# Linear attention into a Swish feed-forward block: one output tile moved ahead of a batch's key-value products, one weight load and one minimum cut in two

## The chip, the cores and the metric

The kernel runs on one NeuronCore of a Trainium2 chip. The metric is the device time of one launch in microseconds (us). A core has five engines that run their own instruction streams and meet only at semaphores: TensorE (PE; its weight loads are shown apart as PEld), VectorE (DVE), ScalarE (ACT), GpSimd (POOL) and SyncE (SP). Transfers are issued by SP, ACT and POOL. TensorE writes into PSUM, which here is cut into banks of 128 x 512 float32; the other engines copy from there to SBUF.

## The reference

```python
def _attn_ref(q, k, v):                      # 8 batches, 8 heads, 576 rows, 64 columns
    def phi(x):
        return np.where(x > 0, x, np.exp(x) - 1.0) + 1.0
    q_p, k_p = (phi(q), phi(k))
    kv = np.einsum('bhsd,bhse->bhde', k_p, v)
    z = np.sum(k_p, axis=2)
    num = np.einsum('bhsd,bhde->bhse', q_p, kv)
    den = np.einsum('bhsd,bhd->bhs', q_p, z)[..., None] + 1e-06
    return (num / den).astype(np.float32)

def _moe_ref(x, w_in, w_out, beta):          # x: 4608 x 512, d_ff = 2048
    h = x @ w_in
    g = h * (1.0 / (1.0 + np.exp(-beta * h)))
    return (g @ w_out).astype(np.float32)
```

The attention's output, its heads side by side, is the x of the second function. Each batch gives 576 rows: 512 of them make four tiles of 128, and the 64 that are left over (the "odd" rows) of all eight batches are gathered in a ninth block.

## The kernel before

**Stages.** For each of nine blocks of 512 rows the kernel runs an h phase (16 products of 128 columns of w_in with xT, the transposed x of the block, each into its own PSUM bank, each followed by Silu on ACT into g) and a y phase (four output tiles, t = 0 to 3; each sums 16 matmuls of g with w_out in one bank). Beside the phases of block b the attention of a later batch is computed. From batch 2 on this is hung between the matmuls by the tables `sh` and `sy`; batches 0 and 1 are written out by hand, and the change lies there. `tc.manual_schedule()` is set: every engine executes its instructions in the order of the program's text.

**phi.** phi(x) = min(exp(x), max(x, 0) + 1). `phi_part` takes exp on ACT (`e`, four buffers), `phi_relu` the other side on DVE (`r`), `phi_min` the minimum on DVE. `phi_step` calls these for batch 0, with an optional range j0:j1 of the nine row groups.

**Batch 0, up to about 20 us.** q and k are loaded, phi is taken, q is transposed on PE (`q_trans`, copied out by `q_copy`). `z_products` sums phi(k), `kv_direct` makes k^T v, `kv_evac` and `diagonal` copy it out on DVE and ACT, `z_evac` copies z. `numer_mm` makes the numerators in tiles of the pool `num0ps` (two buffers, which z uses first), `x_part` transposes x, and `h0_part` is the h phase's first quarter in pieces; it needs the first quarter of w_in.

**Loads.** POOL issues the loads that change the type from float32 to bfloat16: k and v of batch 0 in halves, w_in in four quarters (L119, L120), then w_out in four quarters, q, k, v of batch 1, and q (`xq`), k (`xk`) and v of batch 2. All of them are in POOL's one queue in this order.

**Batch 1, about 30 to 49 us.** Block 0's y phase holds all four banks of the pool `mmps` as `yps[0]` to `yps[3]`. Its matmuls come in quarters i = 0 to 3 of d_ff (`y_mm(0, t, i, ...)`), with batch 1's attention between: `z_products`, `z_evac`, `kv_direct`, `kv_evac`, `dens`, `numer0` and `x_trans1`. The last quarter, i = 3, is what lies between the pieces of attention (L769 to L781):

```python
    y_mm(0, 0, 3, yps[0])
    for t in range(4):
        numer0(1, t, num0_tile() if t < 2 else miscps.tile([P, 512], F32, tag="misc", name="nps1"))
    ...
    for t in (1, 2):
        for i in range(2):
            y_mm(0, t, 3, yps[t], 256 * i, 256 * (i + 1))
            x = 2 * (t - 1) + i
            x_trans1(x, nc.scalar if x < 3 else nc.vector)
    y_mm(0, 3, 3, yps[3])
```

On ACT the order there is: `phi_part(2, "q", 0)` (exp of the first half of batch 2's q, L768), the copies of x_trans1(0) to (2), exp of both halves of batch 2's k, exp of the second half of q, the table load for Silu, and the Silus of block 1. On DVE: the four scalings of `numer0`, the copy of x_trans1(3), then `y_out` of tiles 0 to 2, `phi_relu` of k, `y_out` of tile 3, and the minima. `y_out` copies a bank to one of three buffers `y_sb` and issues two output transfers of 128 KB on SP.

**Block 1's h phase.** Products 0, 1, 2 and 6 go into the banks of `mmps` that `yps` gave back, 5 into that of product 0, 3 and 4 into the pool `numps` (two buffers, `h_ps2`). Product 6 is followed by `q_odd_trans(1, num_tile("qop"))` (L847): two transposes of batch 1's odd rows into the `numps` buffer of product 3, so that PE must wait for the Silu of product 3.

Of the kernel before, what the change touches and what calls it, by code (L numbers as in the profile page):

```python
# [16 lines left out]
def kernel(  # L17
# [10 lines left out]
    nc = tc.nc  # L28
# [8 lines left out]
    J = S // G  # L37
# [18 lines left out]
    w_in_sb = [consts.tile([P, KC, 512], BF16, name=f"w_in{i}") for i in range(4)]  # L56
# [59 lines left out]

    w_in_v = moe_w_in.rearrange("(c p) f -> p c f", p=P)
    w_out_v = moe_w_out.rearrange("(c p) m -> p c m", p=P)
    for i in range(4):  # L119
        nc.gpsimd.dma_start(out=w_in_sb[i], in_=w_in_v[:, :, i * 512 : (i + 1) * 512])  # L120

    def load_w_out(i):
# [17 lines left out]
    def phi_part(b, a, pr, x, j0=0, j1=J):  # L140

        if j0 == 0:
            st[b, a, pr, "e"] = work.tile([P, 2, J, D], BF16, tag="e", name="e", bufs=4)
        nc.scalar.activation(st[b, a, pr, "e"][:, :, j0:j1], x[:, :, j0:j1], ACTF.Exp)  # L144

    def phi_relu(b, a, pr, x):
        r = work.tile([P, 2, J, D], BF16, tag="r", name="r", bufs=2)
        nc.vector.tensor_scalar(r, x, 0.0, 1.0, ALU.max, ALU.add)  # L148
        st[b, a, pr, "r"] = r
# [16 lines left out]
    def xin(b, a, pr):  # L166
        if b == 0 and a == "q":
            return q0f[:, places(b, pr)]
        return (xk if a == "k" else xq)[b % NX][:, places(b, pr)]
# [7 lines left out]
    def k_quads(b, pr, dst, mov):  # L177

        for j in range(J):
            for h in range(2):  # L180
                for hh in range(2):
                    r = slice(hh * G, (hh + 1) * G)
                    c = slice(h * D, (h + 1) * D)
                    nc.tensor.matmul(  # L184
                        dst[hh][c], st[b, "k"][r, pr, j, c], mov(r, j, h),
                        start=(j == 0), stop=(j == J - 1), skip_group_check=True,
                    )

    def z_products(b, pr, ps):

        for j in range(J):
            for hh in range(2):
                r = slice(hh * G, (hh + 1) * G)
                nc.tensor.matmul(
                    ps[hh][:, 256 + pr : 257 + pr], st[b, "k"][r, pr, j, :], ones[r, 0:1],
                    start=(j == 0), stop=(j == J - 1), skip_group_check=True,
                )

    def z_evac(b, ps):
        for hh in range(2):  # L200
            nc.vector.tensor_mul(
                z0[:, hh], ps[hh][:, 256:258, None].to_broadcast([P, 2, 2]),
                kvmask[:, :, :, 0],
            )

        nc.gpsimd.tensor_copy(
            st[b, "kv"].rearrange("p x a (h e) -> p (x a h) e", h=2)[:, :, D],
            z0.rearrange("p x a h -> p (x a h)"),
        )

    def kv_direct(b, pr, ps):
        k_quads(
            b, pr, [a[:, pr * D : (pr + 1) * D] for a in ps],
            lambda r, j, h: vb[b][r, 2 * pr + h, j, :],
        )

    def kv_evac(b, hh, prs, ps):
        p0, p1 = prs[0], prs[-1] + 1
        nc.vector.tensor_mul(
            st[b, "kv"][:, hh, p0:p1].rearrange("p a (h e) -> p a h e", h=2)[:, :, :, 0:D],  # L220
            ps[hh][:, p0 * D : p1 * D].rearrange("p (a d) -> p a d", a=p1 - p0)[
                :, :, None, :
            ].to_broadcast([P, p1 - p0, 2, D]),
            kvmask[:, p0:p1, :, 0:D],
        )
# [15 lines left out]
    def copy(eng, dst, src):  # L241
        if eng is nc.scalar:
            nc.scalar.copy(dst, src)
        else:
            eng.tensor_copy(dst, src)  # L245

    def q_copy(b, k, t, tp, eng):
        slots = 1 if t == NT - 1 else 2
        tp = tp.rearrange("p (t a h i g) -> p t a h i g", a=2, h=2, i=slots, g=G)
        copy(  # L250
            eng,
            st[b, "qT"][:, t, :, :, 0 : slots * G].rearrange("p a h n -> p (a h) n"),
            tp[:, k].rearrange("p a h i g -> p (a h) (i g)"),
        )
# [170 lines left out]
    def x_trans(b, t, eng, tp):  # L425
        n = P if t < NT - 1 else G
        xv = st[b, "xs", t].rearrange("p i a d -> p (i a d)")
        tp = tp[:, 0 : KC * P].rearrange("p (c t) -> p c t", c=KC)
        for p in range(KC):
            nc.tensor.matmul(  # L430
                tp[:, p, :n], xv[:n, p * P : (p + 1) * P], identity[:n, :n],
                is_transpose=True, start=True, stop=True, skip_group_check=True,
            )
        if eng is nc.scalar:
            nc.scalar.copy(x_dst(b, t), tp[:, :, :n])  # L435
        else:
            eng.tensor_copy(x_dst(b, t), tp[:, :, :n])
# [28 lines left out]
    def mm_tile(name):  # L466
        return mmps.tile([P, 512], F32, tag="mm", name=name)

    def y_mm(b, t, i, yp, c0=0, c1=512):
        for c in range(4):  # L470
            ff = 4 * i + c
            nc.tensor.matmul(  # L472
                yp[:, c0:c1],
                g_sb[b % 2][:, ff, t * P : (t + 1) * P],
                w_out_sb[i][:, c, c0:c1],
                start=(ff == 0), stop=(ff == FC - 1), skip_group_check=True,
            )

    def rows(b, j):
        return out[b * S : (b + 1) * S, :].rearrange("(g j) m -> j g m", j=J)[j]  # L480

    def y_out(b, t, yp, c0=0, c1=512, queues=(nc.sync, nc.sync), copier=nc.vector):
        y_sb = work.tile([P, DM], F32, tag="y_sb", name="y_sb", bufs=3)
        copy(copier, y_sb[:, c0:c1], yp[:, c0:c1])
        for i in range(2):
            dst = rows(b, 2 * t + i) if b < B else rows(2 * t + i, J - 1)
            queues[i].dma_start(out=dst[:, c0:c1], in_=y_sb[i * G : (i + 1) * G, c0:c1])
# [48 lines left out]
    def misc_bf():  # L536
        return miscps.tile([P, 1024], BF16, tag="misc", name="tp")
# [18 lines left out]
    def num0_tile():  # L556
        return num0ps.tile([P, 512], F32, tag="num0", name="nps0")
# [15 lines left out]
    def phi_step(a, pr, f, *r):  # L573
        f(0, a, pr, *((xin(0, a, pr),) if f is not phi_min else ()), *r)
# [18 lines left out]
    phi_step("q", 1, phi_min, 0, 4)  # L593
    phi_step("q", 1, phi_min, 4, J)
    phi_step("k", 0, phi_part)
    phi_step("k", 1, phi_part)
    tps = [misc_bf() for _ in range(2)]
    for i in range(2):
        q_trans(0, (2 * i, 2 * i + 1), tps[i], ())
# [1 line left out]
    q_copy(0, 0, 0, tps[0], nc.vector)  # L601
    phi_step("k", 0, phi_min)
    phi_step("k", 1, phi_relu)
    q_copy(0, 1, 1, tps[0], nc.vector)
    phi_step("k", 1, phi_min)
    for t in (2, 3):
        q_copy(0, t - 2, t, tps[1], nc.scalar)
    nc.scalar.activation(tiny[:, 1:2], warm[:, 0:1], ACTF.Silu)
# [72 lines left out]
    def diagonal(b, hh, p0, ps):  # L681

        for h in range(2):
            r = slice(h * D, (h + 1) * D)
            nc.scalar.copy(
                st[b, "kv"][r, hh, p0:2, h * EA : h * EA + D],
                ps[hh][r, p0 * D : 2 * D].rearrange("p (a d) -> p a d", d=D),
            )
# [52 lines left out]
    yps = [mm_tile("y_ps") for _ in range(4)]  # L741
# [14 lines left out]
    for pr in range(2):  # L756
        z_products(1, pr, zt1)
    z_evac(1, zt1)
    for pr in range(2):
        kv_direct(1, pr, kv1)  # L760
    kv_evac(1, 0, (0, 1), kv1)
    diagonal(1, 1, 0, kv1)
    dps1 = miscps.tile([P, 512], F32, tag="misc", name="dps1")
# [2 lines left out]
    phi_tile(2, "q")  # L766
    phi_tile(2, "k")
    phi_part(2, "q", 0, xin(2, "q", 0))  # L768
    y_mm(0, 0, 3, yps[0])  # L769
    for t in range(4):  # L770
        numer0(1, t, num0_tile() if t < 2 else miscps.tile([P, 512], F32, tag="misc", name="nps1"))

    def x_trans1(t, eng=nc.scalar):
        x_trans(1, t, eng, num0_tile().bitcast(BF16) if t < 2 else misc_bf())

    for t in (1, 2):
        for i in range(2):
            y_mm(0, t, 3, yps[t], 256 * i, 256 * (i + 1))
            x = 2 * (t - 1) + i
            x_trans1(x, nc.scalar if x < 3 else nc.vector)  # L780
    y_mm(0, 3, 3, yps[3])  # L781
    for pr in range(2):
        phi_part(2, "k", pr, xin(2, "k", pr))
    phi_part(2, "q", 1, xin(2, "q", 1))
    for t in range(3):
        y_out(0, t, yps[t])
    for pr in range(2):
        phi_relu(2, "k", pr, xin(2, "k", pr))
    y_out(0, 3, yps[3])
    for pr in range(2):  # L790
        phi_min(2, "k", pr)
    for pr in range(2):
# [110 lines left out]
```

## Time and profile before

| what | before |
|---|---|
| median of 13 runs | 285.74 us (285.27 to 287.99) |
| the profiled execution's own time | 285.39 us |
| its span in the profile | 283.6 us |
| PE busy, matmuls / weight loads | 274.9 us (97%) / 139.2 us (49%) |
| DVE / ACT / POOL busy | 106.4 (38%) / 160.6 (57%) / 36.8 us (13%) |
| granted TensorE clock, mean | 0.999 |
| DMA | 41.03 MB, mean 145 GB/s |

The span is what the profile shows of the execution; 1.8 us of the profiled execution's own time lie around it. Shares of busy time are means over stages with different limits. In the profile's lines a time is in us from the start of the span, "L472" is a line of the kernel, "y_ps<-w_out,g" says what is written from what, and "<-" in brackets names what ended an engine's idle time.

### The profile page before, as it was taken

What the parts mean: (1) busy time and instruction counts of PE and PEld (TensorE: products, weight loads), DVE (VectorE), ACT (ScalarE), POOL (GpSimd) and SP (SyncE); (2) the same over time, 40 slices, a digit from 0 to 9 for tenths busy, and PEclk for the clock granted to TensorE, in tenths of its full rate; (3) what the DMA queues carried; (4) which work ended last, traced back from release to release, by engine and by line L of the source; (5) the groups of instructions that cost most, each with busy time, mean ns of one, the idle gap of its engine ahead of it and who ended that gap; (6) DMA issues with size and microseconds to landing.
All of it is one profiled execution on the core that took longest, in us unless ns stands there. A gap on an engine that the chain in (4) does not pass through costs nothing.

```text
span 283.6 us, 5976 instructions
## 1 busy us (share of the span) xinstructions
PE 274.9 (97%) x2477; PEld 139.2 (49%) x2508; DVE 106.4 (38%) x260; ACT 160.6 (57%) x219; POOL 36.8 (13%) x51
## 2 busy tenths in 40 slices
PE   7899999999999999999999999999999999999994
PEld 2574457444854544454445444544444444444443
DVE  5842677806832474056404740371034100110012
ACT  5778586974786744893388528831750185028500
POOL 8722100314013002300040003000000000000000
PEclk9999999999999999999999999999999999999999
DMA  7999999669999938953998379166303510230033
GB/s 219 204 210 390 249 266 191 154 183 238 198 141 288 145 82 200 273 100 83 147 278 144 67 166 285 34 81 160 76 3 83 121 30 0 63 79 8 0 74 75
DMA packets 51723, 41.03 MB, mean 145 GB/s; under 512 B 31584, under 2 KB 43120, under 8 KB 51696
## 3 DMA queue, kind: packets, MB, share of 16 engines
q1 hardware_dynamic: 38800, 23.61, 36.1%
q0 software_dynamic: 12736, 16.91, 30.6%
q8 instruction: 19, 0.31, 0.5%
q10 hardware_dynamic: 160, 0.13, 0.2%
q14 instruction: 8, 0.07, 0.1%
HBM read 36.71 MB, written 9.44 MB: 163 GB/s over the span
## 4 chain that ended last, share of the span: by engine, by line
PE 81%; DMA 13%; POOL 2%; ACT 1%; issue 1%; DVE 0%; POOLq 0%; ACTq 0%
PE y_ps L472 39%; PE h_ps L454 39%; DMA xq<-in_q_dram 8%; DMA w_in<-in_moe_w_in_dram 5%; PE nps L184 1%; PE nps L309 1%; POOL w_in L120 1%; ACT e L144 1%; ACT xT L435 1%; POOL vf L83 1%; PE kvp L184 0%; PE nps_m L309 0%; POOL xk L83 0%; DVE y_sb L245 0%; POOL identity masks.py:199 0%
## 5 line engine op out<-in xcount | busy, mean ns | idle before, releaser
L462 ACT ACTIVATE g<-h_ps,beta_c 128x512 bf16<-128x512 f32 x144 | 97.8, 689 | 86.9 <-PE h_ps L454 86.4
L472 PE MATMUL y_ps<-w_out,g 128*128 128x512 bf16 (+3 forms) x615 | 125.9, 360 | 1.0 <-issue 0.2
L454 PE MATMUL h_ps<-xT,w_in 128*128 128x512 bf16 x487 | 108.5, 379 | 0.8 <-ACT e L144 0.3
L472 PEld LDWEIGHTS <-g 128*128 128x128 bf16 x632 | 60.7, 98 | 61.1
L454 PEld LDWEIGHTS <-w_in 128*128 128x128 bf16 x560 | 54.5, 98 | 65.5 <-DVE y_sb L245 0.7
L245 DVE COPY y_sb<-y_ps 128x512 f32<-128x512 f32 (+2 forms) x37 | 24.7, 672 | 81.2 <-PE y_ps L472 77.1
L392 DVE TENSOR_SCALAR den<-nps 128x12 f32<-128x12 f32 x12 | 2.0, 164 | 63.0 <-PE nps L309 63.0
L144 ACT ACTIVATE e<-xk 128x1152 bf16<-128x1152 bf16 x16 | 17.8, 1153 | 3.1 <-DVE phi_k L155 1.7
L83 POOL DMA_DIRECT2D xq<-in_q_dram x7 | 5.2, 747 | 89.1 <-DVE phi_k L155 41.8
L144 ACT ACTIVATE e<-xq 128x1152 bf16<-128x1152 bf16 x14 | 15.6, 1155 | 1.4 <-DMA xq<-in_q_dram 1.4
L454 PE MATMUL h_ps<-xT_tail,w_in 128*128 128x512 bf16 x62 | 13.9, 379 | 0.1
L173 POOL CAST vaug<-vf 128x1152 bf16<-128x1152 f32 x10 | 11.2, 1151 | 18.4 <-DMA vf<-in_v_dram 14.6
L155 DVE TENSOR_TENSOR phi_q<-e,r 128x1152 bf16<-128x1152 bf16 (+2 forms) x17 | 11.7, 716 | 2.7 <-ACT e L144 2.4
L383 DVE TENSOR_TENSOR xs<-nps,rden 128x512 bf16<-128x512 f32 (+1 forms) x24 | 12.2, 552 | 0.4
L144 ACT ACT_TABLE_LOAD x6 | 7.7, 1283 | 7.9 <-DMA xq<-in_q_dram 7.8
L155 DVE TENSOR_TENSOR phi_k<-e,r 128x1152 bf16<-128x1152 bf16 x16 | 11.7, 764 | 0.2
L133 PE MATMUL warm_ps<-xT 128*128 128x512 bf16 x20 | 7.5, 534 | 1.8 <-DVE xT L96 1.5
L462 ACT ACT_TABLE_LOAD x6 | 7.7, 1283 | 0.1
L83 POOL DMA_DIRECT2D xk<-in_k_dram x9 | 6.8, 758 | 4.6 <-DMA g<-in_moe_w_out_dram 2.0
L730 DVE TENSOR_SCALAR w_out<-g,rbeta 128x512 bf16<-128x512 f32 x8 | 3.8, 536 | 8.7 <-DMA g<-in_moe_w_out_dram 8.7
L184 PEld LDWEIGHTS <-phi_k 64*64 64x64 bf16 x576 | 5.6, 106 | 2.8 <-issue 2.1
L148 DVE TENSOR_SCALAR r<-xk 128x1152 bf16<-128x1152 bf16 x16 | 6.7, 453 | 0.0
(98 smaller groups left out, 118.1 us busy)
## 6 DMA issues: line engine op xcount, KB each, us to landing
out_dram<-y_sb SPq DMA_DIRECT2D x70, 128.0 KB, 2.4
vf<-in_v_dram SPq DMA_DIRECT2D x5, 1152.0 KB, 6.7
xq<-in_q_dram POOLq DMA_DIRECT2D x7, 576.0 KB, 10.1
xk<-in_k_dram POOLq DMA_DIRECT2D x7, 576.0 KB, 12.2
w_in<-in_moe_w_in_dram POOLq DMA_DIRECT2D x4, 512.0 KB, 12.8
g<-in_moe_w_out_dram POOLq DMA_DIRECT2D x2, 1024.0 KB, 17.8
stage<-in_moe_w_out_dram POOLq DMA_DIRECT2D x2, 1024.0 KB, 20.7
stage<-in_q_dram SPq DMA_DIRECT2D x2, 576.0 KB, 4.0
```

What stands on the lines that cost most here:

```text
L83: return eng.dma_start(out=dst[:, h0 : h0 + n].rearrange("p h j d -> p h (j d)"), in_=rows.rearrange("(i p) e -> p i e", p=P)[:, h0 : h0 + n],
L133: nc.tensor.matmul(warm_ps[:, 0:cols], warm[:, 0:P], warm[:, 0:cols], start=True, stop=True)
L144: nc.scalar.activation(st[b, a, pr, "e"][:, :, j0:j1], x[:, :, j0:j1], ACTF.Exp)
L148: nc.vector.tensor_scalar(r, x, 0.0, 1.0, ALU.max, ALU.add)
L155: nc.vector.tensor_tensor(st[b, a][:, pr, j0:j1].rearrange("p j (h d) -> p j h d", h=2), st[b, a, pr, "e"][:, :, j0:j1].rearrange("p h j d ...
L173: eng.tensor_copy(vaug[b % 2][:, pr, :, :, 0:D], src[:, places(b, pr)].rearrange("p h j d -> p j h d"))
L184: nc.tensor.matmul(dst[hh][c], st[b, "k"][r, pr, j, c], mov(r, j, h), start=(j == 0), stop=(j == J - 1), skip_group_check=True,)
L245: eng.tensor_copy(dst, src)
L383: nc.vector.tensor_mul(out, num, rd[..., None].to_broadcast(list(num.shape)))
L454: nc.tensor.matmul(hp[:, c0:c1], w_in_sb[ff // 4][:, kc, (ff % 4) * P : (ff % 4 + 1) * P], x[:, kc, c0:c1], start=(kc == 0), stop=(kc == K ...
L462: nc.scalar.activation(g_sb[b % 2][:, ff, :], hp, ACTF.Silu, scale=beta_c[:, ff : ff + 1])
L472: nc.tensor.matmul(yp[:, c0:c1], g_sb[b % 2][:, ff, t * P : (t + 1) * P], w_out_sb[i][:, c, c0:c1], start=(ff == 0), stop=(ff == FC - 1), ...
```

## The change

It has four parts. The first quarter of w_in is loaded in two halves of 256 columns. Exp and minimum of the second half of batch 0's k are done in two pieces (row groups 0 to 3 and 4 to 8), and the copy of the second transposed q tile comes after the minimum instead of before it. In batch 1, the last quarter of tile 0, `y_mm(0, 0, 3)`, goes in front of `kv_direct`, and the tile's `y_out` right behind. The last quarters of tiles 1 to 3 are cut and placed anew between `dens`, `numer0` and `x_trans1`, with `y_out(0, 1)` ahead of the transposes' last copy; `y_out(0, 3)` comes ahead of `phi_relu` of k.

```diff
-    for i in range(4):
+    for c0, c1 in ((0, 256), (256, 512)):
+        nc.gpsimd.dma_start(out=w_in_sb[0][:, :, c0:c1], in_=w_in_v[:, :, c0:c1])
+    for i in range(1, 4):
         nc.gpsimd.dma_start(out=w_in_sb[i], in_=w_in_v[:, :, i * 512 : (i + 1) * 512])
...
     phi_step("k", 0, phi_part)
-    phi_step("k", 1, phi_part)
+    phi_step("k", 1, phi_part, 0, 4)
+    phi_step("k", 1, phi_part, 4, J)
...
     phi_step("k", 0, phi_min)
     phi_step("k", 1, phi_relu)
+    phi_step("k", 1, phi_min, 0, 4)
+    phi_step("k", 1, phi_min, 4, J)
     q_copy(0, 1, 1, tps[0], nc.vector)
-    phi_step("k", 1, phi_min)
...
     z_evac(1, zt1)
+    y_mm(0, 0, 3, yps[0])
     for pr in range(2):
         kv_direct(1, pr, kv1)
+    y_out(0, 0, yps[0])
     kv_evac(1, 0, (0, 1), kv1)
...
     phi_part(2, "q", 0, xin(2, "q", 0))
-    y_mm(0, 0, 3, yps[0])
+    y_mm(0, 1, 3, yps[1], 0, 256)
     for t in range(4):
         numer0(1, t, num0_tile() if t < 2 else miscps.tile([P, 512], F32, tag="misc", name="nps1"))
...
-    for t in (1, 2):
-        for i in range(2):
-            y_mm(0, t, 3, yps[t], 256 * i, 256 * (i + 1))
-            x = 2 * (t - 1) + i
-            x_trans1(x, nc.scalar if x < 3 else nc.vector)
-    y_mm(0, 3, 3, yps[3])
+    y_mm(0, 1, 3, yps[1], 256, 512)
+    x_trans1(0)
+    y_out(0, 1, yps[1])
+    for i in range(2):
+        y_mm(0, 2, 3, yps[2], 256 * i, 256 * (i + 1))
+        x_trans1(1 + i)
+    y_mm(0, 3, 3, yps[3], 0, 128)
+    x_trans1(3, nc.vector)
+    y_mm(0, 3, 3, yps[3], 128, 512)
     for pr in range(2):
         phi_part(2, "k", pr, xin(2, "k", pr))
     phi_part(2, "q", 1, xin(2, "q", 1))
-    for t in range(3):
+    for t in (2, 3):
         y_out(0, t, yps[t])
     for pr in range(2):
         phi_relu(2, "k", pr, xin(2, "k", pr))
-    y_out(0, 3, yps[3])
```

The number of matmuls on PE grows by four (one product cut at column 128 of tile 3, in place of the uncut four), the other engines' work by one exp, one minimum and one load issue.

## The prediction

> **What bounds the kernel now.** I read the page first (PE is busy 97% of the span), then the chain of waits, which says where PE was not the limit, then the timeline of each engine around the edited lines, then the DMA view.
>
> ```profile
> PE 81%; DMA 13%; POOL 2%; ACT 1%; issue 1%; DVE 0%; POOLq 0%; ACTq 0%
> ...
> 7.62 15.36 DMA w_in<-in_moe_w_in_dram
> ...
> 23.27 21.82 DMA xq<-in_q_dram
> ...
> 45.17 1.16 ACT e L144
> ...
> 46.36 1.07 ACT xT L435 x2
> ...
> 48.00 1.17 ACT e L144
> ...
> 49.19 6.22 PE h_ps L454 x28
> ```
>
> Columns: start, duration, what. Up to 45 us the chain is the load queue of POOL; at 45.1 it goes to ACT (exp of batch 2's q, copies of xT), at 49.19 to PE, where it stays to the end. So only what moves PE's work after 49 us moves the time. PE itself was busy from 20 to 48 us but for tenths.
>
> Two engines run neck and neck there. The timelines of ACT and PE:
>
> ```profile
> 46.36 1.07 ACT L435 COPY xT<-nps 128x512 bf16<-128x512 bf16 x2
> 47.45 0.59 ACT L435 COPY xT<-tp 128x512 bf16<-128x512 bf16 x1
> 48.00 2.22 ACT L144 ACTIVATE e<-xk 128x1152 bf16<-128x1152 bf16 x2
> ...
> 50.12 1.15 ACT L144 ACTIVATE e<-xq 128x1152 bf16<-128x1152 bf16 x1
> ...
> 51.29 1.28 ACT L462 ACT_TABLE_LOAD   x1
> 52.58 4.16 ACT L462 ACTIVATE g<-h_ps,beta_c 128x512 bf16<-128x512 f32 x7
> ...
> 54.31 0.70 ACT L462 ACTIVATE g<-h_ps,beta_c 128x512 bf16<-128x512 f32 x1
> ```
>
> ACT has no gap from 45.17 to 58. The last row is the fourth Silu (product 3), done at 55.01. PE's first transpose of `qop` needs that buffer and starts at 55.25:
>
> ```profile
> 48.13 0.81 PE L472 MATMUL y_ps<-w_out,g 128*128 128x512 bf16 x3
> ...
> 55.25 0.27 PE L284 MATMUL qop<-identity,phi_q 128*128 128x128 bf16 x2
> ```
>
> A semaphore's way from one engine to the next shows as about 0.05 us (chain: "issue" 0.02 to 0.05), so ACT has 55.25 - 55.01 - 0.05 = 0.19 us to spare. PE's own loss before product 0 is: last y matmul issued at 48.56 (three of 0.216 from 48.13), so 48.78 would be possible, and 49.19 it was: 0.41 us. The waits put it on the bank that `y_out(0, 0)` frees, whose copy runs from 48.46 to 49.14.
>
> ```profile
> PEld L454 <- DVE y_sb L245: 0.7, 1, 0.7
> ...
> ACT e L144 <- DMA xq<-in_q_dram: 1.4, 1, 1.4
> ```
>
> The exp at 48.00 reads batch 2's k. That load was issued at 25.99 and took 21.9 us:
>
> ```profile
> xk<-in_k_dram POOLq DMA_DIRECT2D x1, 576.0 KB, 21.9
> ```
>
> It landed at 47.89, 0.1 us before ACT came to it. Nothing but loads is in flight then: from 41 to 48 us queue q0 alone fills the engines.
>
> ```profile
> DMA packets 1280, 1.46 MB, mean 208 GB/s; under 512 B 35, under 2 KB 1278, under 8 KB 1278
> ...
> q0 software_dynamic: 1278, 1.43, 120.2%
> ```
>
> (Over 100%: packets overlap.) An output transfer put there pushes xk back.
>
> **The change part by part.**
>
> *Tile 0 in front, the tiles recut (PE).* The work is the same but for four more matmuls; PE stays gapless. From z's end at 42.3: tile 0's quarter 4 x 0.216 = 0.86 (its weights are scaled at 42.15, in time), kv 0.73, dens 0.40, half of tile 1 0.43, numerators 16 x 0.054 = 0.87, so they end at 45.6 where they ended at 45.2. Then half tile 1, transposes 0, two halves of tile 2 with transposes 1 and 2, 128 columns of tile 3 (0.22), transposes 3, 384 columns (0.65). Transposes 2 are in PSUM at 47.8 (before: 47.42), transposes 3 at 48.25 (48.08), the last y matmul ends its slot at 48.75. Bank 0 is free since about 44, bank 1 at 48.3, and DVE's last xT copy runs from 48.3 to 48.7. PE can start product 0 at 48.8: **0.4 us earlier**. The gain is real, but PE then meets `qop`, where ACT has only 0.19 to give. Of 0.4 at most 0.19 gets through, and only if ACT is not later.
>
> *DVE.* `y_out(0, 0)` needs 0.68 (the page's mean is 0.672) from 43.3, before `kv_evac` at 44.05, which it does not delay; `y_out(0, 1)` fits from 47.65 to 48.3 between the scalings and the last xT copy. Behind these, DVE's 1.15 us wait at 52.21 for an output buffer goes, so batch 2's minima and the DMA transposes of q that wait for them come about 2 us earlier. I cost it at nothing: PE uses phi_k first at 57.2. The banks change hands too: product 5 now takes tile 3's bank and product 6 waits for the first Silu. With Silu 0 at 52.6 + 0.7 that comes before `qop` and no later.
>
> *ACT.* Nothing is added here, but the copy of transposes 2 ends at 47.8 + 0.59 = 48.4 instead of 48.04. By itself this moves the exp of k by +0.38.
>
> *SP and the DMA engines: "copied out at once".* Two transfers of 128 KB are issued at about 44.0 and 44.6 instead of 49.16. SP has nothing else queued between 2.2 and 49 us, so nothing waits behind them there. But they move while xk does. In before each landed 2.4 us after its issue, so they are over by 47 or 48. What do they cost xk? The trace has a stretch, 117 to 120 us, with both kinds:
>
> ```profile
> q0 software_dynamic: 348, 0.40, 76.6%
> q1 hardware_dynamic: 229, 0.37, 38.7%
> ```
>
> In 3 us q0 moved 0.40 MB, 133 GB/s instead of 208: lost 75 GB/s, for output at 0.37/3 = 123 GB/s. So an output byte costs 0.61 byte of the load: 262 KB x 0.61 / 208 GB/s = **0.77 us**; I take 0.7. The Trainium skill, page DMA: Bandwidth & Descriptors, section Issuing engines are not separate DMA queues, says the same in general: transfers of all issuing engines run on the same 16 DMA engines and interleave. One could hold against it that another queue is another path; then the cost is 0, and the sum is 0.38 - 0.19 = +0.2 instead of what follows. The row at 117 us decides for the rule. Ends: 0, and 1.1, if output packets overlap with nothing: from 50.8 to 55 us 417 of them, alone in the engines, had a share of 87.5%, 16 x 4.2 x 0.875 / 417 = 0.14 us each, and a tile is eight per engine.
>
> *w_in's first quarter in two.* One more POOL issue, 0.76 us. POOL's later issues (w_in 1 to 3, the memset, w_out, xq, xk) come up to 1.3 us later, as each waits for the landing of the one eight places before it; hidden, since the loads take 21 us from issue to landing behind others. What counts is packets: 512 of 1 KB (written) become 1024 of 512 B. From 12.5 to 17.5 us 1025 packets of about 1 KB had a share of 123.2%: 16 x 5 x 1.232 / 1025 = 96 ns; from 41 to 48, 1278 of about 1.15 KB, 105 ns. The line through both has about 21 ns per packet beside the bytes: 512 x 21 / 16 / 1.2 = 0.56 us, if that part does not overlap; 0 if it does. The skill's same page, section Specifications, gives 512 B as the smallest transfer at line rate, so by the rule 0. No row has such packets in the load queue. I take 0.2, as the landings of whole quarters (14.7 and 23.0 for the first and last, 2.8 us a quarter; 2.8 too for xk's 576 KB in as many packets) leave room for both. All later loads, xk too, are late by this.
>
> What it gains: `h0_part`'s first weights waited 0.4 us for w_in (landing 14.7), but the xT copy ahead of it ended at 14.63, so under 0.1.
>
> *The minimum in two.* ACT: two exps took 1.26 where one takes 1.16, +0.1. DVE: 0.82 for two minima where one takes 0.76, +0.06. DVE is gapless from 9.1 to 12.0 and `z_evac` stays behind the moved copy, so the numerators at 12.04 (they wait for z's tile) come 0.06 to 0.16 later, not earlier. With w_in's gain the start-up is worth 0 +- 0.15. Cover: ACT's wait for xq (landing 45.1) and xk; a slower start-up of 0.4 would use it up.
>
> **Sum.** xk lands at 47.9 + 0.7 + 0.2 = 48.8, later than ACT's 48.4, so the exp of k starts at 48.85 instead of 48.00. The Silus follow at +0.85, `qop` at +0.85 - 0.19 = **+0.66 us**, with everything after it on PE. The profiled execution took 285.39 (span 283.6 and 1.8 around): 286.05. The median of before is 0.35 above that execution, so I predict 286.4 for the median. That is +0.23%, within the 0.3% (0.86 us) which is about what a measurement of this kernel can tell from no change.
>
> **The rivals.**
>
> *Balance.* The output tile hides in slack of the queue and small packets cost nothing. Then xT's copy decides: +0.38 - 0.19 = +0.2, 285.95 (285.6 to 286.2). For it: DMA share is an average, and packets overlap. Against: q0's loss at 117 us. Chance 0.2.
>
> *The load queue pays in full (slower).* Place: xk's landing. Price: output 1.1, packets 0.56, so exp of k at 49.6, +1.6 - 0.19 = +1.4: 287.15. It decides from 1.1 us of delay of xk on (exp at 49.05, +0.86). For it: 120% of share leaves no room. Against: the pair of rows at 117 us gives 0.77. With the upper part of the main case: chance 0.25.
>
> *PE's gain gets through.* If `qop`'s wait is not where I read it, the 0.41 us are won: 285.3; 285.0 with 0.3 of start-up. For it: PE is the chain from 49 us. Against: ACT's gapless row. Chance 0.07.
>
> The main case without its upper part has 0.48.
>
> **How the numbers follow.** Within 0.3%: 0.48 + 0.2 + 0.02 of the last rival = 0.70. Slower: 0.25. Faster by over 0.3%: 0.05, since even the whole 0.41 is under the bound and only scatter of the runs would carry it over. Range 285.6 to 287.2: from balance to the full queue; what is left out is PE's gain and more than the full price.
>
> **What would show it.** In the profile after: tile 0's copy on DVE near 43.4 and output issues at 44; product 0 at 48.8; xk landing near 48.8 and exp of k right after it; Silus from 53.4; PE idle before `qop` for about 1 us. If xk lands at 47.9, the queue's part is wrong; if PE has no gap before `qop`, the ACT part is wrong; if product 0 is not before 49, the first step is.

## The result and the profile after

The changed kernel takes 288.68 us in the median (287.48 to 292.2, 11 runs), the kernel before 285.74 in the same session (48 runs): a ratio of 1.0092 [1.0071, 1.0112], 0.9% slower. Run again later it gave 287.97 against 285.91, 1.0078 [1.0055, 1.0101]. Ratios, here and below, are estimates over the fast executions with a 95% interval, not quotients of the medians. The prediction said 286.4 and at most 287.2.

The profiled execution of after is an unusual one: its own time is 285.89 (span 284.1), under each of the other eleven. It shows what the prediction worked out; what it does not show made the loss. So this section has two profiles of the same kernel: first this one, then that of the repeat (e1_after, span 285.8).

The chain's shares by engine in the first profile of after: the load queue is no longer the long first part, PE is nearly everything.

```profile
PE 92%; ACT 2%; DVE 2%; DMA 2%; issue 1%; SPq 0%; ACTq 0%; DVEq 0%
```

The timeline of DVE in it (start, duration, what; in brackets the idle time before and what ended it):

```profile
42.81 0.69 DVE L247 COPY y_sb<-y_ps 128x512 f32<-128x512 f32 x1 [0.67 <-PE y_ps L474]
...
47.10 0.68 DVE L247 COPY y_sb<-y_ps 128x512 f32<-128x512 f32 x1
...
50.03 0.69 DVE L247 COPY y_sb<-y_ps 128x512 f32<-128x512 f32 x1 [1.19 <-DMA out_dram<-y_sb]
```

Tile 0 is copied at 42.81, tile 1 at 47.10. The wait for an output buffer did not go: it is at 48.8 instead of 51.1, still 1.19 us. Why is in the DMA view of 43 to 45 us (issues: KB each, median us to landing):

```profile
out_dram<-y_sb SPq DMA_DIRECT2D x2, 128.0 KB, 5.7
```

Beside the load queue the early transfers take 5.7 us, where outputs of this kernel take 2.6 over the whole page. In this execution xk is late too. The same view for 25 to 27 us:

```profile
xk<-in_k_dram POOLq DMA_DIRECT2D x1, 576.0 KB, 22.8
```

22.8 instead of 21.9: xk lands at 48.47, 0.55 us later (e1_after: 48.53). But the same early output leaves xk on time in e2, e5 and e9 below (47.78, 47.92, 47.66), where the transfers take 5.7 us as well; the same two views of e2:

```profile
xk<-in_k_dram POOLq DMA_DIRECT2D x1, 576.0 KB, 21.6
...
out_dram<-y_sb SPq DMA_DIRECT2D x2, 128.0 KB, 5.7
```

There it is the load behind xk, batch 2's v, that lands later (51.25 to 51.54 for 50.76 in before). And e10, without an early output, has xk at 48.31. So that the output is what delays xk in the two profiles of after is not shown. Where xk is late, ACT waits for it, and PE waits for ACT:

```profile
47.44 0.60 ACT L437 COPY xT<-tp 128x512 bf16<-128x512 bf16 x1
48.55 2.22 ACT L146 ACTIVATE e<-xk 128x1152 bf16<-128x1152 bf16 x2 [0.50 <-DMA xk<-in_k_dram]
...
53.13 4.16 ACT L464 ACTIVATE g<-h_ps,beta_c 128x512 bf16<-128x512 f32 x7
```

```profile
48.30 5.35 PE L456 MATMUL h_ps<-xT,w_in 128*128 128x512 bf16 x23
53.87 1.02 PE L456 MATMUL h_ps<-xT,w_in 128*128 128x512 bf16 x4 [0.21 <-ACT g L464]
55.61 0.27 PE L286 MATMUL qop<-identity,phi_q 128*128 128x128 bf16 x2 [0.71 <-ACT g L464]
```

Product 0 starts at 48.30 instead of 49.19, and 0.21 + 0.71 is lost again before `qop`, which ends up 0.36 later than before (55.61 for 55.25). Block 2 then starts at 79.17 instead of 78.70, and the span is 0.5 longer. Had all executions been like this one, the median would have been near 286.2 (an estimate: 285.74 and these 0.5).

They are not. PE's timeline at the start of block 2, in e1_after:

```profile
75.74 3.55 PE L474 MATMUL y_ps<-w_out,g 128*128 128x256 bf16 x31
80.85 1.45 PE L456 MATMUL h_ps<-xT,w_in 128*128 128x512 bf16 x6 [1.57 <-DVE r L150]
```

and in before:

```profile
75.75 3.11 PE L472 MATMUL y_ps<-w_out,g 128*128 128x256 bf16 x27
78.70 3.62 PE L454 MATMUL h_ps<-xT,w_in 128*128 128x512 bf16 x15
```

PE stands for 1.57 us, some 25 us after the last edited step, and block 2 begins 2.15 later than before, which is the whole difference of the spans (285.77 and 283.62). The DVE reciprocal that the line names is only what came last by the records; what block 2's first product needs is `xT`, which four DMA transposes write. This is the view of that tile from 66 to 82 us, in e1_after:

```profile
L444 SPq DMA_TRANSPOSE xT<-xs x4: 1190/1490/2023, 67.8 to 73.7; - x4
...
DMA to landing us min/median/max: 7.1/8.0/9.4
```

and in before:

```profile
L442 SPq DMA_TRANSPOSE xT<-xs x4: 1190/1602/1827, 67.4 to 73.5; - x4
...
DMA to landing us min/median/max: 4.7/7.1/8.8
```

The minimum is the fourth transpose, issued last (73.66, 73.55): it lands at 80.76 instead of 78.26. In before PE came to it at 78.70 with 0.4 us in hand, which no view of waits shows, as nothing waited.

A second thing differs: the mean granted TensorE clock of a run. In the first session 8 of the 11 runs behind the median are under 0.996, in e1_after 12 of 22, in before 22 of 211 beside the experiments. The ten e1 runs above it take 287.24 to 287.85, the others up to 290.86.

### The profile page after: what moved, and what is told of

Same layout as the page of the kernel before. It is cut to its first block, busy times and chain, and to the rows that moved or that the text cites. A ratio compares the mean times of both kernels' runs of the same rounds, so it can differ in the third digit from the quotient of the medians.

```text
span 284.1 us, 5988 instructions
## 1 busy us (share of the span) xinstructions
PE 274.4 (97%) x2482; PEld 139.1 (49%) x2512; DVE 107.9 (38%) x261; ACT 160.8 (57%) x220; POOL 38.7 (14%) x52
## 4 chain that ended last, share of the span: by engine, by line
PE 92%; ACT 2%; DVE 2%; DMA 2%; issue 1%; SPq 0%; ACTq 0%; DVEq 0%
PE y_ps L474 44%; PE h_ps L456 42%; DMA stage<-in_q_dram 2%; PE nps L186 1%; PE h_ps L669 1%; ACT g L464 1%; PE nps L311 1%; PE kvp L186 1%; DVE phi_k L157 1%; PE nps_m L311 0%; ACT e L146 0%; ACT L464 0%; PE nps L635 0%; DVE r L150 0%; PE tp L659 0%
## 5 line engine op out<-in xcount | busy, mean ns | idle before, releaser
L474 PE MATMUL y_ps<-w_out,g 128*128 128x512 bf16 (+4 forms) x621 | 126.5, 359 | 0.9 <-issue 0.2
L146 ACT ACTIVATE e<-xk 128x1152 bf16<-128x1152 bf16 (+2 forms) x17 | 17.9, 1096 | 2.6 <-DMA xk<-in_k_dram 2.5
L157 DVE TENSOR_TENSOR phi_k<-e,r 128x1152 bf16<-128x1152 bf16 (+2 forms) x17 | 12.5, 771 | 0.2
L135 PE MATMUL warm_ps<-xT 128*128 128x512 bf16 x20 | 6.7, 483 | 1.8 <-DVE xT L96 1.5
L150 DVE TENSOR_SCALAR r<-xq 128x1152 bf16<-128x1152 bf16 x14 | 6.8, 518 | 1.0 <-DMA xq<-in_q_dram 1.0
```

The costliest lines, as they stand in the source:

```text
L135: nc.tensor.matmul(warm_ps[:, 0:cols], warm[:, 0:P], warm[:, 0:cols], start=True, stop=True)
L157: nc.vector.tensor_tensor(st[b, a][:, pr, j0:j1].rearrange("p j (h d) -> p j h d", h=2), st[b, a, pr, "e"][:, :, j0:j1].rearrange("p h j d ...
L474: nc.tensor.matmul(yp[:, c0:c1], g_sb[b % 2][:, ff, t * P : (t + 1) * P], w_out_sb[i][:, c, c0:c1], start=(ff == 0), stop=(ff == FC - 1), ...
```

## The experiments

Times are medians; the kernel before was run in the same sessions (285.9 in each). "Low clock" counts runs under 0.996. The other columns are of one profile each. Fetch is when the packet with PE's next instruction block starts (explained with e6), landing that of batch 2's fourth x transpose, wait PE's idle time before block 2.

| kernel | us | ratio [95%] | fetch | landing | wait | low clock |
|---|---|---|---|---|---|---|
| e1_after | 287.97 | 1.0078 [1.0055, 1.0101] | 78.58 | 80.76 | 1.57 | 12 of 22 |
| e2_y_only | 287.76 | 1.0069 [1.0046, 1.0092] | 78.68 | 80.77 | 2.19 | 11 of 22 |
| e3_w_only | 286.55 | 1.0003 [0.9972, 1.0034] | 80.95 | 79.16 | 0.34 | 5 of 14 |
| e4_min_only | 285.71 | 0.9976 [0.9958, 0.9993] | | | | 1 of 22 |
| e5_y_uncut | 286.63 | 1.0023 [1.0006, 1.0039] | 81.31 | 79.40 | 0.54 | 4 of 22 |
| e6_extra_pe | 287.22 | 1.0033 [1.0013, 1.0052] | 77.94 | 79.99 | 1.29 | 4 of 22 |
| e7_y_late | 287.83 | 1.0075 [1.0046, 1.0103] | 78.90 | 80.96 | 2.37 | 4 of 10 |
| e8_y_uncut_late | 286.14 | 1.0005 [0.9989, 1.0020] | 81.28 | 79.28 | 0.65 | 1 of 14 |
| e9_after_less_idle | 287.62 | 1.0047 [1.0033, 1.0061] | 81.20 | 79.30 | 0.70 | 19 of 22 |
| e10_extra_pe32 | 287.53 | 1.0068 [1.0044, 1.0092] | 78.25 | 80.43 | 1.33 | 4 of 16 |
| e11_cand | 286.39 | 1.0012 [0.9991, 1.0034] | 80.50 | 78.84 | 0.41 | 1 of 14 |
| e12_cand_t3 | 285.55 | 0.9984 [0.9967, 1.0001] | 80.59 | 78.51 | 0.08 | 2 of 22 |
| e14_after_t3 | 285.98 | 0.9995 [0.9969, 1.0021] | 79.66 | 79.60 | none | 3 of 14 |
| e15_less_idle_no_w | 287.73 | 1.0048 [1.0029, 1.0067] | 81.75 | 79.88 | 0.87 | 14 of 15 |

e4's profile is of its one low-clock run (0.756, 363.32 us), so it has no entries. e13 is e9's kernel once more, one run, for a profile at a lower clock.

Runs at 0.996 or more alone show the loss without the lower clock. Their middle lies over that of before's such runs by 1.69 us in e1, 1.70 in e2, 1.87 in e7, 1.19 in e6 and 1.56 in e10; by 0.40 to 0.70 in e5, e8, e9 (three runs) and e11; by 0.11 in e3; and 0.02, 0.21 and 0.33 under it in e14, e4 and e12. They fall into the same groups as the waits.

**e1 to e4: after again, and each of its three parts alone.** e2 has only batch 1's new order and the early output; e3 only

```diff
-    for i in range(4):
+    for c0, c1 in ((0, 256), (256, 512)):
+        nc.gpsimd.dma_start(out=w_in_sb[0][:, :, c0:c1], in_=w_in_v[:, :, c0:c1])
+    for i in range(1, 4):
```

and e4 only the last minimum (with its exp) in two pieces.

> The changed kernel again. Queue-and-ACT theory (as predicted): the profile's own 0.5 us is all there is, median 286.2 to 286.4, and the 288.7 of the first session was the chip. Clock theory: the median stays 2 to 3 us over the kernel before and the mean granted TensorE clock of the runs lies under 0.995. Load theory (the small packets or the early output make the loads late by more in most executions than in the profiled one): the median stays 2 to 3 us over, at a clock of 1.0.

> Only the recut of block 0's last quarter and the early output of tile 0 (w_in in one piece, the minimum in one piece). Queue-and-ACT theory: +0.3 to +0.7 us. If the early output carries the loss: +2 to +3 us. If the loss is in the other two parts: within 0.7 us of the kernel before.

> Only w_in's first quarter in two halves. Queue-and-ACT theory: 0 to +0.3 us. If the small packets or the extra load issue carry the loss: +2 to +3 us.

> Only exp and minimum of the second half of batch 0's k in two pieces, the q copy behind. Queue-and-ACT theory: 0 to +0.15 us, hidden. If the loss comes from a different start of PE (its clock): +2 to +3 us with a mean clock under 0.995.

e2 holds nearly all of the loss. e3 is within noise, e4 if anything faster (0.24% by the ratio, 0.2 us between the medians). So the start-up edits are not where it went. e2's `qop` is even earlier than before's (55.06, after a wait of 0.39; its xk landed at 47.78), so the loss of e2 is not at ACT and xk at all, but in its 2.19 us before block 2. And e1, whose `qop` is 0.61 later, starts block 2 at the same time (80.85, e2 80.86): what was lost at `qop` went into a shorter wait there and cost nothing.

**e5, e7, e8: cut or uncut, early or late output.** These three vary e2. Uncut keeps tile 3's last quarter whole, late puts the two copies behind `x_trans1(0)` and the last xT copy:

```diff
# e5 against e2
-    y_mm(0, 3, 3, yps[3], 0, 128)
     x_trans1(3, nc.vector)
-    y_mm(0, 3, 3, yps[3], 128, 512)
+    y_mm(0, 3, 3, yps[3])
# e7 against e2 (e8: both)
-    y_out(0, 0, yps[0])
     kv_evac(1, 0, (0, 1), kv1)
...
     x_trans1(0)
-    y_out(0, 1, yps[1])
+    y_out(0, 0, yps[0])
...
-    for t in (2, 3):
+    for t in (1, 2, 3):
         y_out(0, t, yps[t])
```

> As the recut alone (e2), early output kept, but tile 3's last quarter in one piece: PE has as many instructions as before the change. Fetch theory (eight more PE instructions bring PE's next 16 KB instruction fetch forward, from 80 to about 78.6 us, where it holds up one DMA engine just as batch 2's x transposes land): the fetch is back at 80 us, block 2's first product waits under 0.5 us, median +0.3 to +0.6 us. Load theory (the early output makes xk late, with it batch 2's phi, the loads behind it and so the x transposes): as e2, +1.7 to +2.2 us with a wait of 1.5 to 2.2 us at 80.8.

> As the recut alone (e2), tile 3 cut, but tile 0 is copied out only after the four scalings (near 47.1 us) and tile 1 after the last xT copy, so the first output transfer is issued at 47.8 instead of 43.5. Both theories: xk lands at 47.9 again, ACT is gapless, qop waits less, the 0.4 us of that are gone. Load theory: the wait at 80.8 goes too, median -0.2 to +0.2 us. Fetch theory: it stays, +1.3 to +2 us.

> Both: tile 3 in one piece and tile 0 copied out after the scalings. Both theories: xk at 47.9, no new wait at 80, PE's earlier start of block 1 counts as far as ACT's spare time goes: -0.2 to +0.1 us.

The cut decides: e2 and e7 (cut) lose 0.7%, e5 and e8 (uncut) 0.2 and 0.05%. The early output costs at most 0.2% (e5 against e8) and nothing that shows beside the cut (e2 against e7). So what was named in the change's first words is the small part, and four more matmuls are the large one, though the two pieces of tile 3 (0.22 and 0.65 us by the prediction) take no more of PE's time than the whole (0.86). e8 missed its expectation a little: a wait of 0.65 us was left, and 0.25 us of time.

**e6, e10: only more PE instructions.** Before, with warm-up matmuls added in the start-up, where PE waits anyway: four in e6, sixteen in e10.

```diff
     nc.scalar.activation(tiny[:, 1:2], warm[:, 0:1], ACTF.Silu)
     idle(3)
+    idle(4, 64)      # e10: idle(16, 64)
```

> The kernel before with four 64-column warm-up matmuls more in PE's pause at 9.1 us (eight more PE instructions, nothing on any path there). Fetch theory: the fetch comes at about 79 us, and the wait at block 2's first product and most of the loss appear, +1 to +2 us. Load theory: no change, within 0.3 us.

> The kernel before with sixteen 64-column warm-up matmuls more at 9.1 us (32 more PE instructions). Fetch theory: the fetch is asked for some 3 us before block 2, near 76 us, and is through before the last x transposes come; the wait is shorter than with eight more instructions (1.3 us), +0 to +0.6 us. If every added PE instruction costs alike: about four times what eight cost, or more than +1 us.

e6 has such a wait too, with nothing moved and no output early:

```profile
80.08 3.18 PE L454 MATMUL h_ps<-xT,w_in 128*128 128x512 bf16 x13 [1.29 <-DVE r L148]
```

What differs from before is in the DMA view. PE's instructions come over a queue of their own, about 16 KB a time (the page has 19 packets and 0.31 MB of "q8 instruction"). e6 from 77.5 to 79.2 us:

```profile
q8 instruction: 1, 0.02, 3.9%
```

e1_after, the same stretch:

```profile
q8 instruction: 1, 0.02, 3.6%
```

Before has none there; it has it from 80 to 82 us:

```profile
q8 instruction: 1, 0.02, 3.5%
```

3.9% of 16 engines over 1.7 us is 1.06 us of one DMA engine. With the fetch at 77.9 to 78.9 the fourth transpose lands at 80.0 to 81.0 in five kernels (e1, e2, e6, e7, e10); with the fetch at 79.6 or later it lands at 78.3 to 79.9 in all the others. Sharper is the step from the third landing to the fourth, which leaves out when the group as a whole comes: 2.63 to 2.70 us in those five, 1.17 to 1.32 in the eight profiles that issue the transposes in the same order and fetch late (before, e3, e5, e8, e9, e11, e13, e15). So the fetch goes with some 1.35 us. The first profile of after is the one exception: fetch 77.86, step 1.07, landing 78.30, and there it was the next transfer, a tail transpose, that landed late (80.04; 78.44 in before). After the packet, which ends at 79.22 in e10, this is all that its DMA engines start from 79.2 to 80 us:

```profile
DMA packets 34, 0.01 MB, mean 10 GB/s; under 512 B 34, under 2 KB 34, under 8 KB 34
```

A few packets one after another, and the fourth landing at 80.43: this looks like one engine that works off what it was kept from, with the others waiting for it; which engine a packet is on, no view tells. Why eight instructions (a matmul has its weight load) move the fetch by two us shows in before's row for block 2's first line, PE's sequencer:

```profile
L454 PEldq EVENT_SEMAPHORE  x2: 51/736/1422, 76.8 to 76.9; - x2
```

The sequencer comes to the wait for `xT` at 76.9 and stands there for 1.42 us, until the transpose has landed. In before the request would lie a few instructions behind this wait: it cannot go out before the transposes are done, and so never meets them. Eight instructions more, anywhere ahead, put it in front of the wait. This reading fits on which side of the wait each fetch falls; the request itself is in no record.

e10 was meant to push the fetch well ahead of the transposes, to 76, and missed. Its 32 instructions moved the fetches of 56.70 and 69.32 to 55.04 and 67.83, but the one in question fell at 78.25, later than e6's with only eight. So how far ahead of its use a block is requested is not understood. Its expectation was wrong, its result (+0.68%) fits the table.

**e9, e15: after with PE's count restored.** Two groups of warm-ups fewer (behind `z_products(0, 0)` and `kv_direct(0, 1)`), so that PE has as many instructions as in before; e15 also has w_in's first quarter whole.

```diff
     z_products(0, 0, zt)
-    idle(2)
...
     kv_direct(0, 1, kvp0)
-    idle(2)
```

> The changed kernel less four of batch 0's warm-up matmuls (the two behind z_products, the two behind kv_direct): PE has as many instructions as before the change, everything else of the change stays. Fetch theory: the fetch goes back behind block 2's first product (81 us), the wait there falls from 1.6 us and more to under 0.7, median +0.4 to +0.9 us over the kernel before. Load theory: no difference to the changed kernel, +2 us.

> The kernel of e9 with w_in's first quarter in one piece again. If the halves of w_in are what leaves PE idle long enough in the start-up to lose its clock, at most 5 of 22 runs are under 0.996 and the median is 286.3, ratio 1.001 to 1.002. If the missing warm-ups do it by themselves, most runs stay under 0.996 and the ratio stays at 1.004 or more.

The fetch is back at 81.20 and the wait down to 0.70:

```profile
79.39 3.83 PE L456 MATMUL h_ps<-xT,w_in 128*128 128x512 bf16 x17 [0.70 <-issue]
```

Block 2 starts 1.46 us earlier than in e1 (79.39 for 80.85). The three runs of e9 at full clock take 286.10 to 286.29, against 287.24 to 287.85 for after; that is some 0.4 over before, where the fetch theory had put the median. But 19 of 22 runs are at a lower clock, so the median stays at 287.62. e15 shows the same with w_in whole (14 of 15): the halves of w_in are not what brings it, the two missing warm-ups are enough. Of its two expectations the second holds.

**e13, and e7's profile: where the clock goes.** e7's profile is of a run at 0.992. Its stretches (length; busy time and instructions of PE, PEld, DVE, ACT, POOL; granted clock; DMA share; GB/s):

```profile
core 0: us, PE busy (x) PEld busy (x) DVE busy (x) ACT busy (x) POOL busy (x), PEclk, DMA share, GB/s
76.00:78.70 2.70, 2.69 (x25) 2.16 (x23) 0.93 (x2) 1.31 (x2) 0.00 (x0) 1.00 1.26 193
78.70:81.00 2.30, 0.00 (x0) 0.00 (x0) 1.88 (x4) 2.19 (x2) 0.00 (x0) 1.00 1.53 104
81.00:81.50 0.50, 0.39 (x2) 0.24 (x4) 0.50 (x2) 0.00 (x0) 0.00 (x0) 1.00 1.12 241
81.50:84.90 3.40, 3.40 (x9) 1.25 (x9) 0.38 (x1) 1.37 (x2) 1.23 (x2) 0.52 1.05 221
84.90:87.00 2.10, 2.10 (x11) 0.89 (x10) 0.00 (x0) 1.30 (x2) 0.26 (x1) 0.97 0.97 295
```

PE stands from 78.7 to 81, and right behind that its clock is half for 3.4 us: nine products where full speed gives about sixteen. The span is 287.7; e2, the same wait at full clock, has 285.8. So the wait is paid twice in such a run: 2.4 us of it, and some 1.9 behind it.

e13 tells where e9's kernel, which has no such wait, loses its clock.

> The kernel of e9 once more, for a profile of an execution at a lower clock (19 of its 22 runs were under 0.996). Theory start-up: the half clock follows PE's idle tenths between 6 and 12 us (two warm-up groups fewer and w_in in halves leave PE idle there), so the stretches of some 3.4 us near 0.5 lie between 8 and 18 us and cost 1 to 2 us there. Rival block 2: it follows the wait at 78 to 81 us, as in e7, and lies between 80 and 86 us. Second rival: it is spread, with no stretch near 0.5.

```profile
core 0: us, PE busy (x) PEld busy (x) DVE busy (x) ACT busy (x) POOL busy (x), PEclk, DMA share, GB/s
...
10.00:12.00 2.00, 1.50 (x73) 1.34 (x75) 1.90 (x7) 1.98 (x5) 1.57 (x3) 1.00 1.30 200
12.00:14.00 2.00, 1.42 (x60) 1.22 (x61) 1.14 (x6) 1.39 (x5) 0.88 (x2) 1.00 1.43 198
14.00:14.50 0.50, 0.30 (x2) 0.13 (x2) 0.50 (x3) 0.20 (x1) 0.50 (x1) 0.54 1.27 205
14.50:17.50 3.00, 2.87 (x27) 2.68 (x27) 1.39 (x4) 1.43 (x5) 0.86 (x2) 0.51 1.24 207
17.50:18.00 0.50, 0.50 (x12) 0.50 (x11) 0.05 (x1) 0.28 (x1) 0.00 (x0) 1.00 1.23 205
```

It is the start-up: half clock from 14.0 to about 17.4 after two stretches in which PE was busy for 75 and 71% by the records, with no gap of over half a us; before has 82% and 90% there. The share by itself does not decide it: e15's profile has 67 and 72% there at full clock, and matmul records can be missing. What is shown is that half clock becomes frequent without these two groups of warm-ups. This run took 286.96, about 0.8 more than e9's at full clock (1 to 2 were expected); it has no wait before block 2, where e9 has its 0.70, so part of the cost is taken back there. One stretch of 3.4 us at half speed makes a mean of 1 - 0.5 x 3.4 / 285 = 0.994 (this run's 0.991 has another 1.5 us at the end of the span, behind PE's last work), and e9's low runs gather at 0.994 (eight) and 0.987 to 0.988 (nine): by this estimate one and two such stretches.

How often it happens goes with the wait at block 2 where the warm-ups are whole: 27 of 54 runs with a wait of 1.57 or more (e1, e2, e7), 8 of 38 at 1.3 (e6, e10), 6 of 50 at 0.65 or less with w_in whole (e5, e8, e11).

The Trainium skill, page TensorE: Matmul & The Clock Gate, Part 1: The HAM clock gate, has this: half rate when idle, decided over a free-running window of about 3.4 us. Half rate and length agree with these rows, and a window that runs freely would explain why only some executions of one kernel are hit; no run here shows the window itself. Its limit (section HAM oscillation: no idle gaps over about 3.4 us) is too wide for these runs: in e7 half clock came right behind a gap of 2.4 us, in e13 in a start-up without a gap of over half a us.

**e11, e12, e14: the transposes out of the way.** e11 takes the parts that cost nothing (uncut, late output, minimum in two, w_in whole). e12 is e11, and e14 is after, with one line changed: batch 2's fourth transpose is issued with the other three, ahead of block 1's first output.

```diff
-                at(sy, t // 3 + (2 if b == 1 else 0), lambda t=t: x_trans_dma(n, t))
+                at(sy, (t // 4 + 2 if b == 1 else t // 3), lambda t=t: x_trans_dma(n, t))
```

> Tile 3 uncut, tile 0 copied out after the scalings, and the minimum in two pieces; w_in in one piece. Fetch and ACT theory: -0.5 to +0.1 us (qop 0.15 earlier, what is left is batch 2's x transposes).

> As e11, and batch 2's fourth x transpose is issued with the other three, ahead of block 1's first output tile on SP. If the wait at block 2's first product is for that transpose's landing: it lands 0.6 us earlier, the wait of 0.5 to 0.65 us goes, and the median is 0.3 to 0.7 us under e11.

> After, with batch 2's fourth x transpose issued with the other three, ahead of block 1's first output. Theory landing: the fetch no longer meets the transpose that PE waits for; the wait at block 2 goes from 1.6 us to under 0.3, block 2's first h product from 80.85 to about 79.2, and executions at full clock take 286.0 to 286.4. If all lower clocks come from the wait at block 2, they become rare (at most 3 of 22) and the median is 286.2, ratio 1.001. If they come from the start-up, about half of the runs stay under 0.996 and the median is 287, ratio 1.004. Rival: the fetch delays whatever transfer is there, then the wait stays over 1 us.

e14 shows what the loss hangs on, the landing of that one transpose. The whole change with this one line takes 285.98, 2.0 us less than after without it, and has no wait at block 2:

```profile
76.83 3.33 PE L474 MATMUL y_ps<-w_out,g 128*128 128x256 bf16 x29
80.00 3.19 PE L456 MATMUL h_ps<-xT,w_in 128*128 128x512 bf16 x13
```

(It starts at 80.00 because this profile had its half clock from 12.0 to 15.5, mean 0.994. So the missing wait is better read from e12, at full clock: 0.08. In e14 the early fetch, at 79.66, met the tail transposes instead: they land at 82.0, 2.4 us behind the fourth.) Its runs at full clock have a middle of 285.86, after's 287.6: 1.7 for a wait of 1.57. Its low runs are 3 of 14 where after has 12 of 22, so much of after's lower clock seems to go with the wait; the runs are few. The one low run that was profiled has its half clock in the start-up.

e11 is level with before, not up to 0.5 us under it as expected; a wait of 0.41 was left. e12 is the fastest, 0.16% under before with an interval that touches 1; it beats after clearly, before not surely.

## Why the prediction was wrong

*Right, by its own steps.* PE to product 0: predicted 0.4 earlier, 0.9 in the profile (0.7 in e2, without the start-up edits). Not getting through `qop`: right; 0.92 is lost there in two waits. xk late: predicted 0.7 for the output and 0.2 for small packets, measured 0.55; exp of k predicted at 48.85, measured 48.55; `qop` predicted +0.66, measured +0.36, in e1_after +0.42. The profile that shows only this part has 285.89 as its own time, where the sum said 286.05. But this agreement is in part luck: with the same early output xk is on time in e2 and e9, and `qop` starts there 0.19 and 0.17 earlier than before, neither the main case nor the balance that was put at +0.2. And the price of 1.1 for the rival was too high by its own view: the share of 87.5% is of 529 packets, not of the 417 large ones alone.

*Mis-sized.* Small packets of w_in: I took +0.2 where a rule said 0. From the landing ahead of it the first quarter takes 2.62 to 2.67 us in the six profiles with halves and 2.48 to 2.61 in the others, so about 0.1. Nothing of it reaches later loads: e3, whose queue starts as before's does, has xq at 34.06 for 34.07 and xk at 47.91 for 47.92. Here the figure that the prediction quotes from the Trainium skill, page DMA: Bandwidth & Descriptors, section Specifications, 512 B as the smallest transfer at line rate, was nearer than my line through two rows. The start-up, 0 +- 0.15: in after's profile the numerators come at 11.65 for 12.04, but there the very first load of k, which no edit touches, landed at 7.31 for 7.88, so this is no gain of the edit. e4's medians say 0.2 us, e11 over e8 says nothing.

*Wrong, on the side.* DVE's wait for an output buffer was to go; it only moved, because I gave the early transfers 2.4 us (the page's median) where they took 5.7 beside the load queue, of which I had just said that it filled the engines. And with it batch 2's transposes of q were not 2 us earlier (phi_q ended at 57.08 for 56.83).

*The step that failed* is the last half-sentence of the sum, "with everything after it on PE", together with "The work is the same but for four more matmuls; PE stays gapless". I costed the four matmuls by their time on PE and took all stages behind block 1 as moving along unchanged. Two things were left out. The matmuls are also eight instructions, which shift every later instruction fetch of PE against the data flow, and one of 19 came to lie beside the transpose that block 2 waits for. Block 2 started 2.15 us later (e1), 1.57 of it as a wait. This is shown by e6 (a wait of 1.29 appears with four dummy matmuls alone), e9 (it falls to 0.70, block 2 1.46 earlier, with the count restored) and e14 (the loss goes with the transpose moved). And about half of the runs of kernels with a wait of that size (27 of 54) are at a lower clock, which the sum, made against one profile at full clock, has no term for; that half clock follows the wait itself is shown by one profile, e7's. The rival that was to be slower, the queue paying in full, was not it: e2 and e7 have xk on time (47.78 and 47.94) and lose the same.

*Could it have been seen?* Not the collision's size. But before's margin was there to read: fourth landing 78.26, PE at 78.70, so 0.4 us in hand at a place that the delay at `qop` and every change of PE's count reach.

*Open.* That the 16 KB packet itself holds up the transpose on its engine is argued from the times in these profiles; no run here leaves the fetch out. Why xT lands 0.9 to 1.1 later than in before's one profile even with a late fetch (e3, e5, e8, e9: 79.2 to 79.4) is not settled. It is the whole group that comes later (third landing 78.10 in e5, 77.09 in before), and wherever the transposes are issued in this order, the first lands within half a us of batch 4's k, which is loaded beside them (e5 77.05 and 77.27, before 76.23 and 76.02). About 1 us of e1's later landing is of this kind too (third 78.13), so not all of the 2.5 is the fetch's.

## What to carry to other kernels

Count an added PE instruction twice: its time, and its place in the instruction stream; then look where each later fetch will fall, above all before a wait on a DMA transpose with little margin. For each stage behind the edit ask what it waits for and how long ago that landed: a margin of 0.4 us is a bound that no wait shows. Keep PE's idle time out of the middle of a kernel, and take no warm-up away in a sparse start-up without looking at the granted clock of many runs, since one profile may show none of it.

## What the runs showed of the hardware

- A fetch of PE's instructions, one packet of 16 KB that took about 1 us, went with a later landing of the DMA transpose in whose flight it fell: 2.63 to 2.70 us behind the one before it in five kernels, 1.17 to 1.32 with a late fetch. The Trainium skill, page Runtime: NRT & Kernel Launch, section Instruction fetch mechanics, gives blocks of 16 KiB, 256 instructions, fetched over a queue of the sequencer's own, and calls the cost of a boundary mostly hidden. In before that holds: after 20 us PE has no wait of over 0.26 us.
- 3.4 us at half clock came right behind a PE gap of 2.4 us (e7, some 1.9 us of time) and in a start-up with two groups of warm-ups fewer (e13, about 0.8), in some executions only; without these warm-ups 33 of 37 runs (e9, e15) were at a lower clock.
- Outputs of 128 KB that were issued beside a busy load queue took 5.7 us to land instead of 2.4 to 2.6 (after, e2, e5, e9). In two profiles the load in flight was 0.55 and 0.61 us later, in e2, e5 and e9 it was not, and the load behind it was.
